# A chunk sum of the attention weights' exps by an accumulating DMA instead of VectorE, with a new order of the work

## The chip, the cores and the metric

One core of one Trainium2 chip. The metric is the device time of the kernel in microseconds (us): 325.75 us, the median of three runs (325.48 to 327.68). A core has five engines that the kernel programs: TensorE (PE in the profile, with its weight loads as PEld), VectorE (DVE), ScalarE (ACT), GpSimd (POOL) and SyncE (SP). Each runs its own instructions in the order in which they were written and waits on semaphores for the others. DMAs are issued by POOL, SP and ACT.

## The reference, cut to what matters

Attention with 16 extra "beacon" keys, then a feed-forward layer with an ELU, over 8 batches, 8 heads, 576 queries, head size 64:

```python
k_all = np.concatenate([beacon_k, k], axis=2)          # 16 + 576 keys
v_all = np.concatenate([beacon_v, v], axis=2)
scores = scale * np.matmul(q, k_all.transpose(0, 1, 3, 2))
scores = np.where(causal, -1000000000.0, scores)       # the beacons are seen by all
scores = scores - scores.max(-1, keepdims=True)
a = np.exp(scores)
a /= a.sum(-1, keepdims=True) + 1e-09
attn = np.matmul(a, v_all)
x = attn.transpose(0, 2, 1, 3).reshape(B * S, H * D)   # 4608 x 512
h = x @ w_in                                           # 512 x 2048
g = np.where(h > 0.0, h, np.exp(np.minimum(h, 0.0)) - 1.0)
return g @ w_out                                       # 2048 x 512
```

What the change touches is `a.sum(-1)`, the denominators of the softmax.

## The kernel before, in words

**The order is a list of words.** The kernel defines steps (`S`, `x`, `m`, `D`, `L` and so on) and then runs a long string of words such as `D.4.0.1` (lines 831 to 958), one step with its arguments each. The order of the words is the order of the instructions on every engine; nothing is reordered afterwards. A word that ends in `.v` runs on VectorE what its plain form runs on ScalarE; one that ends in `.d` gives to a DMA what its plain form gives to VectorE.

**Attention.** For batch b the 592 keys are cut into five chunks of up to 128 (`kc`), and because of the causal mask chunk j is needed only for queries from `ilo[j]` on: 0, 112, 240, 368, 496. So the scores of one head have 576 + 464 + 336 + 208 + 80 = 1664 columns (keys on partitions, queries along the columns). `S` (line 307) multiplies keys with queries into PSUM, `x` (line 328) takes the exp on ScalarE into the tiles `et`, of which there are three in rotation, one per batch and group of four heads. `m` (line 345) zeroes the masked corners on VectorE: part 0 in chunks 0 and 1, part 1 in chunks 2 to 4.

**The denominators.** A sum over keys is a sum over partitions and over chunks. `D.b.d.n` (line 390) adds the chunks of head group d (d = 0 or 1) on VectorE into one tile of fp16, `presum`, which lies in `qkp` and exists once: n = 0 adds chunks 0 and 1 (128 x 1856 elements over four heads), n = 1 adds chunk 2 to that (128 x 1344), n = 2 chunk 3 (128 x 832), n = 3 chunk 4 (80 x 320). `L` (line 408) then multiplies the result with a block of ones on TensorE (line 426); where there is no presum it multiplies each chunk (line 377). `n` (line 436) turns the sums into reciprocals with Ln and Exp on ScalarE, `W` (line 455) multiplies the exps with v, and `M` (line 485) scales the result into `xT` on VectorE. Batches 3 to 7 have `D` for both groups, batch 2 for one, eleven groups in all.

The branch that the change uses is there already, at lines 397 to 400:

```python
if eng == "d":
    nc.gpsimd.dma_start(out=o, in_=t[0:rows, :, col:col + e - a], accum_op=ALU.add)
    return
nc.vector.tensor_tensor(
```

**The feed-forward layer.** Tokens are taken in ten tiles (0 to 9; 256 columns for 0 and 1, then 512). In tiles 0 to 5 `F` (line 509) is four products of 512 columns (L518) that give one bank of h; `e` (L528) takes exp on ScalarE, `u` (L534 on ScalarE, L536 with `.v`) the ReLU, and `k` (L548) joins both on VectorE into `gt`. `r` and `g` (L555, L560) do the same as `u` and `k` by two VectorE instructions. There are two banks for h, so the next `F` but one waits until `e` and `u` have read the bank. Tiles 6 to 9 use a seven-product scheme for the same layer: `P` (L732), `K` (L746, L749), `E` (L760), `U` (L767, L769), `V` (L777), with `X` and `H` making its operands. The second layer uses such a scheme in tiles 1 to 9: `Z` makes combinations of `gt`, `Q.t.a.b` runs products a to b of 112 (L625), `J` copies the results out of PSUM and sends them off. `Z.t.1.B.d` (L571) already is an accumulating DMA in SBUF, of 512 KB; in tiles 3 to 8 some `J` add into the output with an accumulating DMA (L656).

**Queues.** POOL issues the loads of q, k and v (`lq`, `lv`, `lk`), of the weights (`wi`, `wo`) and all accumulating DMAs; `lp` are small copies on POOL. `lk` puts q or k of a later batch into DRAM as bf16, and `lt` (SP, L808) reads it back with a transpose. SP issues most outputs.

Of the kernel before, what the change touches and what calls it, by code (L numbers as in the profile page):

```python
# [17 lines left out]
def kernel(  # L18
# [813 lines left out]
    warm.1 lq.0.0.0.4 warm.1 warm.1 lq.0.1.0.4 warm.4 warm.1 lq.0.0.4.8 warm.1 warm.4 ident  # L832
    warm.1 bt bk T.0.0.0 cb.0.1 warm.1 cb.0.0 cb.0.2 warm.1 ck.0.0.0 lq.0.1.4.8 T.0.1.0 S.0.0.0
    T.0.0.1 cq.0.1.0 S.0.1.0 x.0.0.0 warm.1 cq.0.0.1 T.0.1.1 S.0.0.3 x.0.1.0 T.0.3.0 S.0.0.2
    cq.0.1.1 x.0.0.3 T.0.2.0 cq.0.3.0 lq.1.0.0.4 x.0.0.2 S.0.1.3 x.0.1.3 cb.0.3 warm.1 S.0.1.1
    x.0.1.1 T.0.2.1 S.0.1.2 tri cb.1.1 m.0.0.3 warm.1 x.0.1.2 S.0.3.0 cq.0.2.0 cq.0.2.1 T.0.3.1
    S.0.2.3 lv.0.2 warm.1 lv.0.0.1 x.0.3.0 m.0.3.0 m.0.0.0 x.0.2.3 S.0.2.0 m.0.1.0 x.0.2.0
    m.0.2.0 S.0.0.1 x.0.0.1 wi.2 S.0.2.2 x.0.2.2 L.0.A cb.1.0 T.1.0.0 cq.1.0.0 T.1.1.0 n.0.A
    cq.0.3.1 m.0.2.2 warm.4 S.0.2.1 W.0.A.0 ck.1.1.0 S.0.3.2 lv.0.3.4 x.0.2.1 m.0.1.2 x.0.3.2
    M.0.A.0 W.0.A.1 S.0.3.1 x.0.3.1 wi.1 m.0.2.3 M.0.A.1 S.1.1 cb.1.2 x.1.1 m.0.1.3 m.0.0.2  # L840
    S.0.3.3 F.0.4 x.0.3.3 m.0.3.3 S.1.4 x.1.4 m.0.3.2 e.0.4 L.0.B W.0.B.0 u.0.4.v k.0.4 n.0.B
    S.1.3 F.0.2 M.0.B.0 x.1.3 lq.1.0.4.8 F.0.3 S.1.0 u.0.3.v u.0.2.v W.0.B.1 x.1.0 T.1.2.0
    M.0.B.1 e.0.3 F.0.5 lq.2.0.0.4 m.1.0.0 e.0.2 ck.1.2.0 cb.1.3 T.1.3.0 e.0.5 k.0.2 S.1.6
    cq.1.3.0 wi.0 F.1.5 S.1.2 u.0.5 x.1.6 e.1.5 k.0.3 x.1.2 S.1.5 cb.2.0 k.0.5 F.1.4 S.1.10
    u.1.5.v k.1.5 x.1.5 H.1.0 u.1.4 e.1.4 F.1.2 x.1.10 u.1.2.v k.1.4 e.1.2 T.2.0.0 F.0.1 S.1.7
    e.0.1 wi.3 lv.1.0.1 cq.2.0.0 F.0.0 x.1.7 T.2.1.0 u.0.0 S.1.12 r.0.1 g.0.1 e.0.0 lq.2.0.4.8
    cq.2.1.0 x.1.12 F.1.0 m.1.0.1 cb.2.1 e.1.0 u.1.0.v S.1.11 S.1.9 x.1.11 F.0.6 x.1.9 k.1.2
    u.0.6.v S.1.8 x.1.8 F.1.6 lv.1.2.3.4 e.0.6 k.1.0 u.1.6.v T.2.3.0 T.2.2.0 ck.2.3.0 cb.2.3
    F.0.7 k.0.0 wo.1 S.2.10 e.1.6 F.1.1 cb.2.2 cq.2.2.0 m.1.1.0 m.1.1.1 k.1.6 L.1.0 u.0.7 wo.2
    x.2.10 e.0.7 k.0.7 n.1.0 L.1.1 lp.3.1 M.1.0.0 n.1.1 k.0.6 F.1.3 lp.3.0 M.1.1.0 W.1.1 M.1.1.1  # L850
    e.1.3 u.1.1 W.1.0 u.1.3 M.1.0.1 e.1.1 S.2.4 x.2.4 F.1.7 F.2.8 wo.0 k.1.3 u.1.7 e.1.7 S.2.1
    k.1.1 u.2.8 e.2.8 k.1.7 lp.4.0 S.2.3 x.2.3 wt.1.0 F.2.13 F.2.7 u.2.7 wo.3 S.2.5 k.2.8 lk.3.0
    u.2.13 x.2.1 Z.1.3.B Q.1.0.7 Q.1.7.14 Z.1.1.B lk.3.1 lk.4.0 e.2.7 e.2.13 k.2.7 Q.1.14.21
    Q.1.21.28 x.2.5 Z.1.2.B wt.2.0 J.1.0 F.2.5 e.2.5 S.2.11 wt.3.0 lv.2.0.1 u.2.5 k.2.5
    lv.2.2.3.4 wt.1.1 S.2.6 lk.4.1 wt.2.1 Q.1.28.35 x.2.6 x.2.11 F.2.1 F.2.3 e.2.3 S.2.8 lk.5.0
# [131 lines left out]
```

## Time and profile before

| | |
|---|---|
| median of three runs | 325.75 us |
| the profiled execution's own time | 325.44 us |
| its span in the profile | 323.7 us |
| PE, DVE, ACT, POOL busy | 315.3, 291.9, 291.3, 116.1 us |
| granted TensorE clock | 1.00 of full speed |
| L400, the chunk sums on DVE | 11 each of four shapes: 1118, 849, 585 and 316 ns |

In the views of the profile L400 means line 400 of the kernel. "Busy" counts the time in which an engine executes; DMA issues take time of the engine that issues them. A row of a group gives engine, operation, output and inputs with their shapes, the count, and behind the bar the busy time in us and the mean of one in ns, then the idle time before them and what ended it. A row of the view of DMAs gives the issuing queue, the count, the size of one and the us from its issue to its landing.

### The profile page before, as it was taken

The page shows a single profiled execution, that of the slowest core. Times are in us where ns is not written, and L with a number is a line of the kernel's source. Part 1 is how long each engine was busy: PE and PEld are TensorE (multiplying, and loading weights), DVE is VectorE, ACT ScalarE, POOL GpSimd, SP SyncE. Part 2 cuts the span into 40 slices and gives each one's busy share as a digit, 9 for nine tenths or more (in the row PEclk, how much of TensorE's full clock was granted, in tenths as well). Part 3 has the DMA queues.
Part 4 walks back from the last instruction along what each step waited for, and adds up shares of the span by engine and source line. Part 5 has one row for each costly group of instructions (what it writes and reads, how often), then busy time and mean ns, then how long its engine had stood idle before and what let it go on. Part 6 is the DMA issues. An engine that isn't in the chain of part 4 may idle for free.

```text
span 323.7 us, 9046 instructions
## 1 busy us (share of the span) xinstructions
PE 315.3 (97%) x3705; PEld 224.0 (69%) x3708; DVE 291.9 (90%) x533; ACT 291.3 (90%) x485; POOL 116.1 (36%) x133
## 2 busy tenths in 40 slices
PE   8889999999999999999999999999999999999995
PEld 3557776656556656555655568788888888888884
DVE  2776999999979999989998999999999998989963
ACT  2998999999799999999999998999999999998930
POOL 8984729545247300550155061310401211131110
PEclk9999999999999999999999999999999999999999
DMA  9999999999999999599999992923484292374345
GB/s 113 179 186 204 185 201 165 159 139 172 141 171 174 174 140 177 68 132 148 195 134 136 166 116 62 146 53 93 61 141 99 35 130 59 90 111 73 97 99 130
DMA packets 141657, 42.53 MB, mean 131 GB/s; under 512 B 113200, under 2 KB 141616, under 8 KB 141616
## 3 DMA queue, kind: packets, MB, share of 16 engines
q0 software_dynamic: 106976, 26.35, 90.3%
q1 hardware_dynamic: 33920, 15.34, 24.9%
...
## 4 chain that ended last, share of the span: by engine, by line
PE 83%; ACT 8%; DVE 5%; issue 2%
PE ops L625 29%; PE hps L518 18%; PE hps L732 11%; PE sc L319 6%; PE ut L377 5%; ACT et L334 5%; PE sa L732 4%; PE sx L625 2%; PE w L205 2%; PE lt L377 1%; ACT e L528 1%; DVE gt L573 1%; PE lt L426 1%; DVE qkp L400 1%; PE ub L377 1%
## 5 line engine op out<-in xcount | busy, mean ns | idle before, releaser
L334 ACT ACTIVATE et<-sc 128x1024 f16<-128x1024 f32 (+2 forms) x114 | 104.1, 973 | 3.9 <-PE sc L319 3.5
L625 PEld LDWEIGHTS <-gt 128*128 128x128 f16 x864 | 83.2, 98 | 16.3 <-issue 1.3
L518 PE MATMUL hps<-xT,w_in 128*128 128x512 f16 (+1 forms) x384 | 79.1, 345 | 0.6 <-ACT e L528 0.4
L656 POOL DMA_DIRECT2D out_dram<-osb x18 | 22.0, 1224 | 127.1 <-ACT osb L649 65.8
L518 PEld LDWEIGHTS <-w_in 128*128 128x128 f16 x384 | 34.5, 98 | 28.8 <-issue 5.4
L625 PE MATMUL ops<-w_out,gt 128*128 128x256 f16 x416 | 54.1, 273 | 0.0
L625 PE MATMUL ops<-wt,gt 128*128 128x256 f16 x400 | 52.4, 273 | 0.0
L528 ACT ACTIVATE e<-hps 128x512 f32<-128x512 f32 x80 | 48.6, 625 | 2.1 <-PE hps L518 2.1
L548 DVE SCALAR_TENSOR_TENSOR gt<-e,r 128x512 f16<-128x512 f32 x73 | 48.8, 684 | 1.7 <-ACT e L528 0.8
L777 DVE SCALAR_TENSOR_TENSOR gt<-e,r 128x512 f16<-128x512 f32 x64 | 42.6, 683 | 1.9 <-ACT e L760 1.5
L149 POOL DMA_DIRECT2D v<-in_v_dram x40 | 38.6, 1270 | 7.8 <-issue 4.4
L534 ACT ACTIVATE r<-hps 128x512 f16<-128x512 f32 x55 | 33.1, 627 | 1.4 <-PE hps L518 1.4
L339 DVE TENSOR_TENSOR et<-et,triu 128x1024 f16<-128x1024 f16 (+5 forms) x66 | 26.5, 447 | 2.1 <-ACT et L334 2.1
L760 ACT ACTIVATE e<-qst 128x512 f32<-128x512 f32 x40 | 26.0, 657 | 1.5 <-DVE qst L749 1.5
L732 PEld LDWEIGHTS <-w_in 128*128 128x128 f16 x256 | 24.4, 98 | 4.2 <-issue 0.4
L573 DVE TENSOR_TENSOR gt<-gt 128x2048 f16<-128x2048 f16 (+1 forms) x24 | 25.9, 1084 | 0.2
L377 PEld LDWEIGHTS <-v 128*32 128x32 f16 (+1 forms) x800 | 17.5, 97 | 9.0 <-issue 1.4
L749 DVE TENSOR_TENSOR qst<-hps,kst 128x512 f32<-128x512 f32 x32 | 21.7, 684 | 0.7 <-ACT kst L746 0.6
L377 PE MATMUL ut<-et,v 128*32 128x464 f16 (+3 forms) x560 | 20.9, 296 | 0.1
L571 POOL DMA_DIRECT2D gt<-gt x6 | 9.9, 1658 | 27.2 <-DVE gt L548 20.2
L746 ACT COPY kst<-hps 128x512 f32<-128x512 f32 x32 | 18.7, 603 | 1.1 <-PE hps L732 1.1
L400 DVE TENSOR_TENSOR qkp<-qkp,et 128x1344 f16<-128x1344 f16 (+2 forms) x33 | 19.2, 583 | 0.4
...
## 6 DMA issues: line engine op xcount, KB each, us to landing
out_dram<-sm SPq DMA_DIRECT2D x18, 256.0 KB, 2.7
out_dram<-osb POOLq DMA_DIRECT2D x18, 256.0 KB, 4.3
out_dram<-osb SPq DMA_DIRECT2D x17, 256.0 KB, 5.2
v<-in_v_dram POOLq DMA_DIRECT2D x24, 128.0 KB, 10.5
gt<-gt POOLq DMA_DIRECT2D x6, 512.0 KB, 7.0
scr<-in_q_dram POOLq DMA_DIRECT2D x5, 576.0 KB, 19.8
scr<-in_k_dram POOLq DMA_DIRECT2D x5, 576.0 KB, 21.4
w_in<-in_moe_w_in_dram POOLq DMA_DIRECT2D x8, 256.0 KB, 8.6
```

The lines of the kernel that those rows point to most:

```text
L149: nc.gpsimd.dma_start(out=vt[b][r0:r0 + n, j, :, :], in_=v[b, :, ilo[j]:ilo[j] + n, :].rearrange("h s d -> s h d"),)
L334: nc.scalar.activation(out=ets[b, d][:, :, a - EC2 * d:e - EC2 * d], in_=sc[b, g][:, :, a - c0:e - c0], func=AFT.Exp, bias=0.0, scale=SCALE)
L339: nc.vector.tensor_tensor(out=o, in0=o, in1=i, op=ALU.mult)
L377: nc.tensor.matmul(out=t[32 * i:32 * (i + 1), a - qa:e - qa], lhsT=ones[0:kc[j], :] if half is None else v16[0:kc[j], j, h, half:D:2], rhs ...
L518: nc.tensor.matmul(out=h[:, n_, :], lhsT=w_in16[:, cc, P * fc:P * (fc + 1)], rhs=xt[k][:, cc, a - TT * k:e - TT * k], start=(cc == 0), sto ...
L528: nc.scalar.activation(out=eb[t, i], in_=flat(hp[t, i]), func=AFT.Exp, bias=0.0, scale=1.0)
L534: nc.scalar.activation(out=rb[t, i], in_=flat(hp[t, i]), func=AFT.Relu, bias=0.0, scale=1.0)
L548: nc.vector.scalar_tensor_tensor(out=half(t, i), in0=eb[t, i], scalar=1.0, in1=rb[t, i], op0=ALU.subtract, op1=ALU.min)
L573: (nc.vector if eng == "v" else nc.gpsimd).tensor_tensor(out=o_, in0=a_, in1=b_, op=op_)
L625: nc.tensor.matmul(out=half_of(xy[t, n_], qd), lhsT=lw[:, P * qd:P * (qd + 1)], rhs=wt_[:, c, :], start=(first and c == 0 and (qd == 0 or ...
L732: nc.tensor.matmul(out=hx[t, g, n_][:, c, :], lhsT=lw, rhs=rh, start=(first and c == 0 and k_ == 0), stop=(k_ == 1), skip_group_check=True)
L777: eng.scalar_tensor_tensor(out=o_, in0=v_(eb[t, g, ph]), scalar=1.0, in1=v_(rb[t, g, ph]), op0=ALU.subtract, op1=ALU.min)
```

## The change

Eight words get a `.d`: `D.4.0.1`, `D.4.1.1`, `D.5.0.1`, `D.5.1.1`, `D.6.0.1`, `D.6.1.1`, `D.7.0.1`, `D.7.1.1`. So in batches 4 to 7 chunk 2 of each head group is added by a DMA that POOL issues. The functions are unchanged. The whole list of words is new: the same steps in another order, and some with another engine. Counted over the lists: `u` on ScalarE 55 before and 51 after, `u.v` 18 and 23, `r`/`g` pairs 7 and 6, `k` 73 and 74, `U` 40 and 41, `U.v` 24 and 23, `J` and its `.v` forms with one more on VectorE, and one of the first copies out of PSUM by ScalarE (`ck.0.1.0`) instead of VectorE (`cq.0.1.0`). The lines around batches 4 and 5:

```diff
-    Q.2.91.98 M.3.1.1 u.3.11 e.3.11 M.3.1.0 D.4.0.0 S.5.4 x.5.4 S.4.7 x.4.7 Q.2.98.105 F.4.3
-    S.5.3 S.4.9 k.3.1 J.2.5 e.4.3 u.4.3 D.4.0.1 D.4.0.2 Q.2.105.112 D.4.0.3 F.3.15 k.3.12 k.4.3
...
-    Q.3.35.42 x.5.9 x.5.10 m.4.1.1 m.4.1.0 k.4.14 D.4.1.0 u.4.4 u.4.15 e.4.15 Q.3.42.49 S.5.0
-    S.5.5 F.4.0 k.4.4 F.4.6 lt.6.1 x.5.5 x.5.0 e.4.6 W.4.1 u.4.0 H.4.2 e.4.0 D.4.1.1 D.4.1.2
-    D.4.1.3 H.4.0 k.4.15 J.3.2 L.4.1 m.5.0.1 Q.3.56.63 m.5.0.0 Q.3.63.70 u.4.6 k.4.6 n.4.1
...
+    Q.2.77.84 J.2.4 u.3.0 F.3.4 k.3.13 u.3.4 D.4.0.1.d lp.6.0 Q.2.84.91 F.3.15 e.3.4 M.3.1.0
+    M.3.1.1 k.3.0 F.3.11 e.3.15 u.3.15 S.4.9 S.4.11 F.3.12 lk.6.0 lt.5.1 lp.5.1 x.4.9 Q.2.91.98
+    u.3.11.v k.3.15 S.4.12 u.3.12.v x.4.11 e.3.11 H.4.0 k.3.11 S.5.3 Q.2.98.105 F.4.2 x.4.12
+    e.3.12 k.3.4 D.4.0.2 F.3.1 x.5.3 e.4.2 S.4.8 S.4.7 u.3.1 Q.2.105.112 e.3.1 u.4.2.v F.4.11
...
+    F.4.12 F.4.9 k.4.7 lk.7.0 u.4.9.v D.4.1.0 u.4.12 Q.3.14.21 e.4.12 S.5.11 S.5.7 e.4.9 k.4.12
+    F.4.4 F.4.10 D.4.1.1.d x.5.11 S.5.2 x.5.7 k.4.9 u.4.4.v e.4.10 lv.5 lt.6.0 S.5.0 e.4.4
+    u.4.10.v J.3.0 Q.3.21.28 Z.3.2.B F.4.14 k.4.8 Q.3.28.35 x.5.0 F.4.0 x.5.2 J.3.1 S.5.8 k.4.4
+    S.5.6 k.4.10 D.4.1.2 D.4.1.3 Q.3.35.42 e.4.0 x.5.8 x.5.6 Q.3.42.49 Q.3.49.56 S.5.1 u.4.14
...
+    x.5.1 S.5.10 x.5.10 r.4.0 g.4.0 m.5.0.1 m.5.0.0 Q.3.56.63 F.4.15 L.4.1 e.4.15 D.5.0.0
+    D.5.0.1.d lt.6.1 e.4.14 k.4.14 u.4.15.v W.4.1 J.3.2 F.4.13 n.4.1 M.4.1.0 Q.3.63.70 F.4.6
+    M.4.1.1 J.3.3 lk.7.1 e.4.13 S.6.2 S.5.12 u.4.13 e.4.6 F.4.5 k.4.15 u.4.6 Q.3.70.77 F.4.1
...
+    Q.3.84.91 F.5.13 x.5.9 S.6.3 J.3.4.v x.6.4 x.6.3 S.6.1 k.4.1 F.5.14 Q.3.91.98 D.5.0.2
+    D.5.0.3 m.5.1.0 L.5.0 x.6.1 D.5.1.0 u.5.13 e.5.13 H.4.2 W.5.0 n.5.0 m.5.1.1 F.5.12
+    Q.3.98.105 u.5.14 M.5.0.1 M.5.0.0 e.5.12 e.5.14 Q.3.105.112 u.5.12 X.6.1 F.5.15 k.5.14
+    F.5.10 D.5.1.1.d k.5.12 S.6.9 J.3.5 u.5.15 S.6.6 Z.4.3.B Z.4.1.B.d J.3.6.v e.5.15 F.5.7
...
```

The order of POOL's words in the stretch that has them, before:

```
lk.5.0 lv.3.2.3.4 lv.3.0.1 lp.4.1 lk.5.1 lk.7.0 lp.5.0 lk.6.1 lv.4 lk.6.0 lp.5.1
Z.3.1.B.d lv.5 lk.7.1 lp.6.0 J.3.1 lp.7.0 lp.6.1 J.3.4.v J.3.5 Z.4.1.B.d lv.6
lp.7.1 J.4.1.v lv.7 J.4.4 Z.5.1.B.d
```

and after:

```
lp.3.1 lv.3.2.3.4 lk.5.0 lv.3.0.1 lk.5.1 lk.6.1 lv.4 lp.5.0 lp.4.1 D.4.0.1.d lp.6.0
lk.6.0 lp.5.1 Z.3.1.B.d lp.6.1 lk.7.0 D.4.1.1.d lv.5 J.3.1 D.5.0.1.d lk.7.1 J.3.4.v
D.5.1.1.d J.3.5 Z.4.1.B.d lp.7.0 lv.6 D.6.0.1.d J.4.1.v lp.7.1 lv.7 D.6.1.1.d J.4.4
Z.5.1.B.d
```

At the start, `ident` comes after the first four loads instead of the first six, and 13 of the `warm` products (matmuls of zeros) stand ahead of `bt` instead of 14.

More of the change, by code (lines that the diff above doesn't have):

```diff
@@ L831 @@
     run("""
[L832 to L855, printed above, removed]
@@ L952 @@
-    V.9.2.4 U.9.3.5 K.9.3.4 E.9.3.1 E.9.3.5 P.9.3.6 V.9.3.1 V.9.3.5 U.9.2.6 Q.8.84.91 U.9.3.4.v
-    J.8.4 Z.9.3.0 Q.8.91.98 Q.8.98.105 Q.8.105.112 E.9.3.6 Z.9.1.0 E.9.3.4 V.9.3.4 U.9.3.6
-    E.9.2.6 V.9.3.6 J.8.6 Z.9.3.1 Q.9.0.7 V.9.2.6 Z.9.1.1 Q.9.7.14 Q.9.14.21 Z.9.2.1 Z.9.2.0
-    Q.9.21.28 J.9.0 Q.9.28.35 J.9.1 Q.9.35.42 Q.9.42.49 Q.9.56.63 Z.9.4.0 J.9.2 Q.9.49.56
-    Q.9.63.70 Q.9.70.77 J.9.3.v Q.9.77.84 Z.9.4.1 J.8.5 Q.9.84.91 J.9.4 Q.9.91.98 J.9.5
+    warm.4 warm.1 lq.0.0.0.4 lq.0.1.0.4 warm.4 ident warm.4 bt bk lq.0.0.4.8 warm.1 warm.1
@@ new lines @@
+    T.0.0.0 ck.0.0.0 warm.1 cb.0.3 cb.0.0 T.0.1.0 ck.0.1.0 S.0.0.0 T.0.0.1 cb.0.1 cq.0.0.1
+    x.0.0.0 S.0.1.0 T.0.1.1 S.0.0.2 cq.0.1.1 T.0.3.0 x.0.1.0 S.0.1.3 T.0.2.0 x.0.0.2 lq.0.1.4.8
+    S.0.1.1 cb.0.2 cq.0.2.0 warm.1 warm.1 lq.1.0.0.4 cq.0.3.0 x.0.1.3 S.0.1.2 T.0.2.1 cq.0.2.1
+    x.0.1.1 lv.0.2 x.0.1.2 S.0.0.3 x.0.0.3 warm.1 warm.1 S.0.3.0 T.0.3.1 x.0.3.0 cq.0.3.1
+    S.0.2.2 lv.0.0.1 x.0.2.2 warm.1 cb.1.1 S.0.2.3 warm.1 x.0.2.3 tri m.0.1.0 S.0.2.0 x.0.2.0
+    m.0.0.3 S.0.3.2 warm.1 S.0.3.1 warm.1 x.0.3.2 x.0.3.1 S.0.0.1 x.0.0.1 S.0.3.3 x.0.3.3
@@ new lines @@
+    K.6.0.5 M.6.0.0 V.6.0.6 J.4.6 P.6.1.1 H.4.3 S.7.3 K.6.1.0 E.6.0.5 S.7.12 x.7.3 P.6.1.2
+    Q.5.0.7 K.6.1.1 V.6.0.1 P.6.1.3 U.6.1.1.v K.6.1.2 S.7.2 P.6.1.4 Q.5.7.14 E.6.1.1 D.6.1.2
+    K.6.1.3 x.7.2 U.6.0.5.v P.6.1.5 D.6.1.3 K.6.1.4 V.6.0.4 V.6.0.5 P.6.1.6 L.6.1 K.6.1.5 x.7.12
+    W.6.1 E.6.1.6 n.6.1 U.6.1.4.v P.6.2.0 U.6.1.6 K.6.2.0 V.6.1.1 Q.5.14.21 E.6.1.4 P.6.2.1
+    E.6.1.5 P.6.2.2 U.6.1.5.v M.6.1.1 M.6.1.0 V.6.1.4 K.6.2.1 J.5.0 S.7.4 K.6.2.2 S.7.5
+    Q.5.21.28 E.6.2.1 x.7.4 P.6.2.4 Z.5.2.B V.6.1.6 P.6.2.3 K.6.2.3 Q.5.28.35 Q.5.35.42 P.6.2.5
@@ new lines @@
+    K.8.2.0 K.8.1.5 P.8.2.1 V.8.0.4 V.8.1.1 J.7.0 P.8.2.2 P.8.2.3 E.8.1.6 E.8.2.1 Q.7.21.28
+    U.8.2.1.v U.8.1.6 U.8.1.5.v K.8.2.2 V.8.1.6 P.8.3.3 P.8.3.0 E.8.1.4 K.8.2.3 Z.7.2.B V.8.2.1
+    U.8.1.4 P.8.2.4 P.8.2.5 K.8.2.5 E.8.1.5 Q.7.28.35 J.7.1 K.8.2.4 E.8.2.5 X.9.1 K.8.3.3
+    K.8.3.0 Q.7.35.42 V.8.1.5 Q.7.42.49 P.8.2.6 E.8.2.6 Q.7.56.63 P.8.3.1 P.8.3.2 U.8.2.4
+    V.8.1.4 Z.7.4.B P.8.3.5 U.8.2.5 K.8.3.2 E.8.2.4 U.8.2.6 Q.7.49.56 J.7.2.v V.8.2.5 Q.7.63.70
+    P.9.0.0 K.8.3.5 V.8.2.4 P.8.3.4 J.7.3.v Q.7.70.77 Q.7.77.84 E.8.3.1 U.8.3.5 K.8.3.4 X.9.2
@@ L957 @@
+    E.9.3.5 V.9.3.5 E.9.3.4 V.9.2.6 Q.8.84.91 Q.8.91.98 P.9.3.6 U.9.3.6 E.9.3.6 Z.9.3.1 J.8.5
+    Q.9.0.7 V.9.3.4 V.9.3.6 Q.8.98.105 Q.8.105.112 J.8.6 Z.9.1.1 Q.9.7.14 Z.9.2.0 Q.9.14.21
+    Z.9.2.1 Q.9.21.28 J.9.0 Q.9.28.35 J.9.1 Z.9.4.0 Z.9.4.1 Q.9.35.42 Q.9.42.49 Q.9.49.56
+    J.9.2.v Q.9.56.63 Q.9.63.70 J.9.3.v Q.9.70.77 Q.9.77.84 Q.9.84.91 J.9.4 Q.9.91.98 J.9.5
     Q.9.98.104 Jh.9.0 Q.9.104.112 Jh.9.1
```

178 lines of the change are left out of this document (87 added, 91 removed).

## The prediction

> **What bounds the kernel now.** I read the page first: engine shares, slices, the chain that ended last.
>
> ```profile
> span 323.7 us, 9046 instructions
> PE 315.3 (97%) x3705; PEld 224.0 (69%) x3708; DVE 291.9 (90%) x533; ACT 291.3 (90%) x485; POOL 116.1 (36%) x133
> ...
> DMA  9999999999999999599999992923484292374345
> ...
> PE 83%; ACT 8%; DVE 5%; issue 2%
> ```
>
> Three engines are near full, TensorE most, and the DMA engines are full up to slice 24 (some 194 us) except for one slice. An average doesn't say where TensorE waits, so the busy time by stretch comes next: start, length, busy us of PE, PEld, DVE, ACT, POOL, then clock, DMA share, GB/s.
>
> ```profile
> 0.00:20.00 20.00, 16.83 (x255) 9.52 (x258) 11.08 (x36) 12.84 (x17) 17.69 (x31) 1.00 1.34 152
> 20.00:40.00 20.00, 19.28 (x371) 13.78 (x371) 16.30 (x37) 18.76 (x28) 13.02 (x21) 1.00 1.46 195
> 40.00:60.00 20.00, 19.43 (x337) 12.87 (x336) 18.72 (x34) 18.79 (x29) 11.22 (x12) 1.00 1.74 178
> ```
>
> ```profile
> 60.00:280.00 220.00, 219.83 (x2388) 152.71 (x2386) 212.11 (x374) 213.13 (x360) 66.73 (x65) 1.00 1.19 126
> ```
>
> ```profile
> 150.00:250.00 100.00, 100.00 (x1124) 73.05 (x1123) 98.44 (x183) 98.33 (x170) 26.86 (x28) 1.00 0.91 117
> ```
>
> ```profile
> 300.00:323.70 23.70, 20.16 (x184) 17.64 (x182) 15.09 (x26) 10.01 (x21) 2.35 (x2) 1.00 0.45 108
> ```
>
> TensorE is idle for 3.2 + 0.7 + 0.6 us in the first 60, for 0.17 us in the next 220, and for 3.5 us in the tail. Busy could hide stalls, so I look at the chain of work around the first affected batches (start, length, what).
>
> ```profile
> 142.93 1.83 PE hps L518 x8
> 144.76 0.76 PE ops L625 x7
> 145.53 0.55 PE sc L319 x12
> ```
>
> Seven L625 products in 0.76 us are 109 ns each; 256 columns at that pace are 2.35 per ns, and the granted clock is 1.00 in every row above. Eight L518 products of 512 columns in 1.83 us are 229 ns each, the same pace with one transition. So from 60 us on TensorE streams at its rate: this kernel is **bound by TensorE**, with VectorE and ScalarE, 98% busy at 150 to 250 us, just able to feed it.
>
> **The change, part by part.** The prices of what leaves and joins VectorE, by group and shape:
>
> ```profile
> L400 DVE TENSOR_TENSOR qkp<-qkp,et 128x1344 f16<-128x1344 f16 x11 | 9.3, 849 | 0.0
> L548 DVE SCALAR_TENSOR_TENSOR gt<-e,r 128x512 f16<-128x512 f32 x73 | 48.8, 684 | 1.7 <-ACT e L528 0.8 <-ACT r L534 0.7
> L536 DVE TENSOR_SCALAR r<-hps 128x512 f16<-128x512 f32 x18 | 12.3, 689 | 4.9 <-ACT e L528 3.2 <-PE hps L518 1.2
> L560 DVE TENSOR_TENSOR gt<-hps,r 128x512 f16<-128x512 f32 x7 | 4.8, 688 | 0.2
> L555 DVE TENSOR_SCALAR r<-e 128x512 f16<-128x512 f32 x7 | 3.6, 521 | 0.1
> L534 ACT ACTIVATE r<-hps 128x512 f16<-128x512 f32 x55 | 33.1, 627 | 1.4 <-PE hps L518 1.4
> ```
>
> *Removed:* eight sums of 128x1344 at 849 ns, 6.8 us of VectorE. *Given back by the new order:* counting words of both lists, five more `u` with `.v` (18 to 23) at 689 ns, +3.4; one `r`/`g` pair fewer, -1.2, and its `k`, +0.7; the other swaps (two `U.v` fewer, one `U.6.v` and one `J.v` more, one `cq` fewer) nearly cancel. VectorE nets some -3.9 us; ScalarE, with four `u` fewer at 627 ns, about -2. TensorE's matmuls are the same in number and shape. Since TensorE lacks only 0.17 us between 60 and 280 us, the relief has almost nothing to buy there: I take **0** of it, bounds 0 and the 0.6 + 0.17 us idle between 40 and 280. What covers the eight sums today is TensorE's stream.
>
> *Added:* eight DMAs of 128 x 1344 x 2 bytes, 336 KB, from SBUF into SBUF with an add, issued by POOL, on the queue that also carries the loads of v, q and k. The trace has no such transfer of this size; the nearest rows (size, median us to landing; then the six 512 KB ones: ns of the issue, and landing min/median/max):
>
> ```profile
> out_dram<-osb POOLq DMA_DIRECT2D x18, 256.0 KB, 4.3
> v<-in_v_dram POOLq DMA_DIRECT2D x24, 128.0 KB, 10.5
> gt<-gt POOLq DMA_DIRECT2D x6, 512.0 KB, 7.0
> scr<-in_q_dram POOLq DMA_DIRECT2D x5, 576.0 KB, 19.8
> scr<-in_k_dram POOLq DMA_DIRECT2D x5, 576.0 KB, 21.4
> ```
>
> ```profile
> L571 POOL DMA_DIRECT2D gt<-gt x6: 1532/1562/2164, 133.4 to 285.6; - x6
> ...
> DMA to landing us min/median/max: 6.4/7.0/10.0
> ```
>
> Between 4.3 us at 256 KB and 7.0 at 512 lies 4.3 + 80/256 x 2.7 = **5.1 us** for 336 KB, an estimate; with the worst `gt` instead, 8.1. POOL's own cost is 8 x 1.6 = 12.5 us of an engine that is 36% busy; it delays nothing but what stands behind it in POOL's order.
>
> The Trainium skill's page "DMA: Bandwidth & Descriptors" (section "Anatomy of one DMA") gives 2.0 us plus bytes over 436 GB/s. By that rule ours would land in 2.8 us, and the 512 KB ones in 3.2; the trace shows 6.4 to 10.0 for these, so the rows decide. By the page no wait would ever appear, and the sum would be the second case below.
>
> *The new wait.* `D.b.d.2` adds into the tile that the DMA writes, so VectorE stops at it until the DMA has landed, and queued behind it are `k`, `u.v` and copies that free TensorE's banks. Prices of TensorE's words, from the chain of work:
>
> ```profile
> 158.44 0.86 PE hps L518 x4
> 191.86 1.32 PE ut L377 x40
> 194.50 0.87 PE hps L732 x8
> ```
>
> An `F` is four L518, 0.86 us; a `P` four L732, 0.44; a `Q` product 0.109; an `S` about 0.45 and a `W` about 1, estimated from the L319 row above and the L377 row, which hold more than one word. Between `D.b.d.0`, after which the DMA can go, and `D.b.d.2` the new list has this much TensorE work: 10.8, 8.5, 12.7, 9.0, 16.0, 10.6, 13.5 and 8.3 us for 4.0, 4.1, 5.0, 5.1, 6.0, 6.1, 7.0, 7.1. By VectorE's words alone it is 7.4, 5.4, 8.0, 7.7, 13.8, 7.4, 11.7 and 7.7. All exceed 5.1, nearly all 8.1. On a free queue this change **waits nowhere**.
>
> The queue isn't free. A tiny transfer behind a large one shows it (issues at 96 to 99 us, and one scr load on a nearly empty queue at 47.4 us):
>
> ```profile
> scr<-in_k_dram POOLq DMA_DIRECT2D x1, 576.0 KB, 23.0
> v<-in_beacon_v_dram POOLq DMA_DIRECT2D x1, 16.0 KB, 21.5
> ```
>
> ```profile
> scr<-in_q_dram POOLq DMA_DIRECT2D x1, 576.0 KB, 11.0
> ```
>
> 16 KB took 21.5 us, because what POOL issued before had to go first. So each new DMA is read with its predecessors in POOL's order: 4.0 follows `lk.5.1 lk.6.1 lv.4`, long issued; 4.1 stands **right behind `lk.7.0`**; 5.0 behind the six pieces of `lv.5`; 5.1 behind `lk.7.1`; 6.0 and 6.1 behind `lv.6` and `lv.7`, but with 16.0 and 10.6 us; 7.0 and 7.1 behind nothing. The critical one is 4.1. Its time in the present run:
>
> ```profile
> 133.38 1.58 POOL L571 DMA_DIRECT2D gt<-gt  x1 [20.23 <-DVE gt L548]
> ```
>
> ```profile
> 148.29 1.11 DVE L400 TENSOR_TENSOR qkp<-et 128x1856 f16<-128x1856 f16 x1
> ```
>
> The new list has four `F`, 28 `Q` products and six `S` less ahead of `D.4.1.0`: 3.5 + 3.1 + 2.7 = 9.3 us, so it starts near 139.0 and ends at 140.1; `D.4.1.2` is then due at 148.6. `lk.7.0` waits behind `Z.3.1.B.d` (133.4 now) and goes at about 135. It lands after 11.0 us (146) to 23.0 (158); our 336 KB behind it add 336/256 x 2.7 = 3.5: 149.5 to 161.5. VectorE is late by 0.9 to 12.9 us; I take 2.5, near the low end, because in the new list the transposing reads and `lv.5`, which run beside the k load at 139 us now, come after `lk.7.0`. TensorE has 21 `Q` products (2.3 us) and two `S` there that ask nothing of VectorE, so about 0.7 us of it passes through. For 5.0 and 5.1, whose margins over 8.1 are 4.6 and 0.9, I add 0.5 together (0 to 3).
>
> *Moved:* everything else. The start is limited by loads and ScalarE:
>
> ```profile
> 10.72 7.67 ACT et L334 x10
> ```
>
> Ten exps in a row there; the new list puts `ident` two DMAs earlier on POOL (earlier first transposes, later second half of the q and k loads), gives ScalarE one more copy (`ck.0.1.0`) ahead of the first exp and has 13 `warm` ahead of `bt` instead of 14. I take 0, bounds -1.5 and +2: the idle 3.2 us of the first row can't all go.
>
> *Sum.* The profiled execution took 325.44 us (span 323.7 and 1.7 around it), 0.3 below the median of 325.75: 325.4 + 0 + 0.7 + 0.5 = **326.6 us**. A change of under 1% (3.3 us) is about what can't be told from none here.
>
> **The rivals.**
>
> *No wait at all (325.3).* All eight DMAs land in time; TensorE's stream sets the end. For it: the margins above; the six `gt` transfers, for which VectorE waits nowhere: the only DMA among what it waited for is the first load.
>
> ```profile
> DVE hi L219 <- DMA lo<-in_beacon_k_dram: 3.7, 1, 3.7
> ```
>
> Against: the scr load just ahead of 4.1. With part of the idle 0.8 us: 324.6 to 325.4. The skill's DMA page, by its 2.8 us, gives this case.
>
> *The queue ahead of 4.1 (331.5, slower).* `lk.7.0` lands as the scr loads mostly do, in 20 to 23 us: 4.1 lands at 158.5 to 161.5, VectorE is 10 to 13 us late. The cover of 2.3 us and 3.9 us of relieved VectorE come off, which leaves 4 to 7, say 5, and 5.0 and 5.1, behind `lv.5` and `lk.7.1` in the same backlog, add about 1: 325.4 + 6 = 331.5, up to 333. It decides from the point where VectorE's wait at `D.4.1.2` exceeds about 6 us, that is, a landing after 154.6.
>
> *The start gains (322.4, faster).* 1.5 us from the start, 0.8 from the idle rest, 0.7 off the tail's 3.5: 325.4 - 3.0. Against: three engines have to be early at once.
>
> *The sums leave VectorE in name only.* VectorE stands at `D.b.d.2` for as long as the sum took (0.85 us each): 6.8 us of waits replace 6.8 of work, and the five added `u.v` make it 3.4 longer than now; TensorE covers most: +1, inside the forecast's range.
>
> **How the numbers follow.** Forecast, with the last rival in it: 0.50, own range 325.0 to 328.9. No wait: 0.15. Queue: 0.27. Start: 0.08. Faster by over 1%: 0.08; within: 0.65; slower: 0.27. The range leaves out the start's gain and the worst of the queue: 323.6 to 332.0.
>
> **What would show it.** Right: L400 of 128x1344 at three instead of eleven; eight new POOL issues into qkp, landing in 5 to 8 us from batch 6 on and later in 4.1; idle time of VectorE before L400 put down to that DMA, under 3 us each; TensorE's 60 to 280 us at 218 or more of 220. Wrong: VectorE waits of 6 us and more, with L518 behind them waiting for e or r; or a first L518 shifted by over 2 us.

## The result and the profile after

The changed kernel takes **331.32 us** (median of 17 runs, 327.01 to 337.80) against 325.75 (17 runs, 325.41 to 327.68). The ratio, with the five longest, disturbed runs of the changed kernel left out, is **1.0105 (95% interval 1.0082 to 1.0129)**: slower by about 1%, just at the bound named in the prediction. The medians over all 17 lie further apart, 1.7%. The profiled execution is the longest of the 17 (337.8 us), so its rows show the loss at its largest; there is no profile of an execution near the median. Run 7 below, whose list behind the start is the same, gives a second look at the same places.

From the page of the changed kernel, the rows that answer to the first ones of before:

```profile
span 336.1 us, 9064 instructions
...
PE 318.5 (95%) x3708; PEld 224.3 (67%) x3708; DVE 289.0 (86%) x531; ACT 289.4 (86%) x479; POOL 127.5 (38%) x141
...
PEclk9999999999999999999999995999999999999999
DMA  9999999999999929999979999963592666466362
...
PE 75%; ACT 9%; DMA 8%; DVE 3%; issue 2%; POOL 2%; ACTq 0%; DVEq 0%; POOLq 0%
```

VectorE lost 2.9 us of work and ScalarE 1.9, POOL gained 11.4. New is the share of DMA in the chain that ended last, 8%, and the one slice (202 to 210 us) with half the TensorE clock. The stretches (start, length, busy us of PE, PEld, DVE, ACT, POOL, clock, DMA share, GB/s):

```profile
20.00:40.00 20.00, 17.66 (x411) 12.99 (x401) 13.31 (x24) 17.72 (x27) 13.29 (x21) 1.00 1.48 194
60.00:150.00 90.00, 90.00 (x946) 53.27 (x945) 83.63 (x141) 86.44 (x136) 34.87 (x36) 1.00 1.64 153
150.00:180.00 30.00, 30.00 (x356) 17.96 (x357) 26.60 (x47) 28.82 (x49) 14.67 (x14) 1.00 1.44 149
180.00:210.00 30.00, 22.39 (x214) 13.55 (x203) 20.21 (x42) 18.90 (x31) 8.12 (x10) 0.89 1.79 134
210.00:280.00 70.00, 69.95 (x780) 58.43 (x778) 68.81 (x126) 67.34 (x124) 18.18 (x14) 1.00 0.66 101
```

So in this execution the loss has two main places. From 20 to 40 us TensorE is busy 17.66 us where it was 19.28: 1.6 us. From 180 to 210 us it is idle for 7.6 us, at a mean clock of 0.89. Between 60 and 180 us, where the DMAs of 4.0, 4.1, 5.0 and 5.1 are, and after 210 us, TensorE is as full as before.

The sums and their DMAs, by group and by line:

```profile
L400 DVE TENSOR_TENSOR qkp<-qkp,et 128x1344 f16<-128x1344 f16 x3 | 2.6, 851 | 0.0
L400 DVE TENSOR_TENSOR qkp<-qkp,et 128x832 f16<-128x832 f16 x11 | 6.5, 587 | 8.5 <-DMA qkp<-et 8.4
...
L536 DVE TENSOR_SCALAR r<-hps 128x512 f16<-128x512 f32 x23 | 15.6, 684 | 1.9 <-ACT e L528 0.9 <-PE hps L518 0.6
```

```profile
L398 POOL DMA_DIRECT2D qkp<-et x8: 1287/1304/1326, 122.5 to 257.8; - x8
...
  DVE qkp L400: 8.4, 4
...
DMA to landing us min/median/max: 4.9/6.7/21.6
```

Eight sums are gone from VectorE, and eight DMAs are there. They land in 4.9 to 8.9 us, all but one: the DMA of 6.0 takes **21.6 us**. Of the 8.4 us that VectorE waits for them, 5.9 are at that one. The waits from 170 to 212 us (in total, times, longest):

```profile
DVE qkp L400 <- DMA qkp<-et: 5.9, 1, 5.9
...
PE lt L426 <- DVE qkp L400: 4.2, 1, 4.2
...
DVE gt L573 <- DMA gt<-gt: 2.0, 1, 2.0
PE ops L625 <- DVE gt L573: 2.0, 1, 2.0
...
PE ut L377 <- DMA v<-in_v_dram: 1.4, 1, 1.4
```

TensorE's three waits add up to the 7.6 us: 4.2 behind the DMA of 6.0, 2.0 behind `gt` and 1.4 for v, and all three transfers are among those of the stretch from 173 to 182 us. What TensorE does around it, in stretches of 5 us (the sixth of the figures after the length is the granted clock):

```profile
195.00:200.00 5.00, 3.57 (x56) 1.84 (x54) 2.42 (x8) 4.46 (x7) 4.78 (x7) 1.00 1.43 131
200.00:205.00 5.00, 0.78 (x24) 0.40 (x16) 1.64 (x6) 0.00 (x0) 0.20 (x1) 0.77 2.23 112
205.00:210.00 5.00, 5.00 (x33) 3.54 (x26) 3.34 (x7) 2.41 (x4) 0.00 (x0) 0.54 1.51 175
210.00:215.00 5.00, 5.00 (x48) 4.47 (x46) 4.41 (x10) 3.64 (x8) 3.86 (x3) 1.00 0.71 73
```

It stands for 4.2 us, and then runs at 0.54 of its clock for 5 us: it looks full there, and does 33 matmuls where the next stretch has 48. At 0.54 those 5 us are worth 2.7, so the slow clock adds 2.3 us to the wait. By the sum 1.6 + 7.6 + 2.3 = 11.5 of the 12.4 us between the two spans are placed.

The 9.9 us at 180 to 210 are those of the longest execution, not the price of this place in the ratio. In the profile of run 7 (328.87 us), with the same order there, the DMA of 6.0 takes 15.1 us, and the stretch costs TensorE 1.5 us at full clock:

```profile
180.00:210.00 30.00, 28.52 (x294) 20.05 (x287) 28.09 (x62) 26.32 (x45) 13.06 (x13) 1.00 1.54 161
```

Why 6.0? The DMAs in flight from 173 to 181 us, changed kernel (size, median us to landing):

```profile
gt<-gt POOLq DMA_DIRECT2D x1, 512.0 KB, 11.9
v<-in_v_dram POOLq DMA_DIRECT2D x3, 128.0 KB, 14.3
...
qst<-scr SPq DMA_TRANSPOSE x2, 13.0
```

and the same transfers from 160 to 175 us in the kernel before:

```profile
gt<-gt POOLq DMA_DIRECT2D x1, 512.0 KB, 10.0
v<-in_v_dram POOLq DMA_DIRECT2D x3, 128.0 KB, 9.4
...
qst<-scr SPq DMA_TRANSPOSE x2, 5.8
```

The difference is on SP's queue. SP from 155 us on, changed kernel, then the kernel before (start, us, what):

```profile
174.14 0.37 SPq L654 DMA_DIRECT2D out_dram<-osb  x1
174.62 6.05 SPq L808 DMA_TRANSPOSE qst<-scr  x2
```

```profile
160.30 4.57 SPq L808 DMA_TRANSPOSE qst<-scr  x2
176.99 0.37 SPq L654 DMA_DIRECT2D out_dram<-osb  x1
```

In the old list `lt.7.0`, the transposing read of batch 7, stands ahead of `J.3.6.v`, whose output SP writes, and runs at 160 us. In the new list it stands behind it, and SP gets to it at 174.6 us: just when POOL issues `gt`, the six pieces of `lv.6` and, at 181.7 us, the DMA of 6.0. That this bunching makes the landing late was a reading so far; the runs test it.

### The profile page after: what moved, and what is told of

The parts are those of the page before. It is cut to its first block, busy times and chain, and to the rows that moved or that the text cites. A ratio compares the mean times of both kernels' runs of the same rounds, so it can differ in the third digit from the quotient of the medians.

```text
span 336.1 us, 9064 instructions
## 1 busy us (share of the span) xinstructions
PE 318.5 (95%) x3708; PEld 224.3 (67%) x3708; DVE 289.0 (86%) x531; ACT 289.4 (86%) x479; POOL 127.5 (38%) x141
## 4 chain that ended last, share of the span: by engine, by line
PE 75%; ACT 9%; DMA 8%; DVE 3%; issue 2%; POOL 2%; ACTq 0%; DVEq 0%; POOLq 0%
PE ops L625 29%; PE hps L518 16%; PE hps L732 11%; DMA qkp<-et 6%; PE sc L319 6%; PE ut L377 5%; ACT et L334 4%; PE sa L732 4%; PE sx L625 2%; DMA kst<-in_k_dram 2%; ACT e L528 2%; PE lt L377 1%; ACT r L534 1%; PE lt L426 1%; POOL qst L136 1%
## 5 line engine op out<-in xcount | busy, mean ns | idle before, releaser
L518 PE MATMUL hps<-xT,w_in 128*128 128x512 f16 (+1 forms) x384 | 80.3, 344 | 0.0
L625 PE MATMUL ops<-wt,gt 128*128 128x256 f16 x400 | 53.4, 273 | 2.0 <-DVE gt L573 2.0
L149 POOL DMA_DIRECT2D v<-in_v_dram x40 | 37.2, 1113 | 10.4 <-issue 5.2
L534 ACT ACTIVATE r<-hps 128x512 f16<-128x512 f32 x51 | 31.0, 623 | 2.7 <-PE hps L518 2.3
L398 POOL DMA_DIRECT2D qkp<-et x8 | 10.4, 1305 | 55.5 <-PE hps L518 24.5
L760 ACT ACTIVATE e<-qst 128x512 f32<-128x512 f32 x40 | 25.2, 646 | 1.7 <-DVE gt L777 0.8
L377 PEld LDWEIGHTS <-v 128*32 128x32 f16 (+1 forms) x800 | 17.1, 97 | 10.6 <-DMA v<-in_v_dram 1.7
L400 DVE TENSOR_TENSOR qkp<-qkp,et 128x832 f16<-128x832 f16 (+2 forms) x25 | 12.5, 500 | 8.7 <-DMA qkp<-et 8.4
```

What stands on the lines that cost most here:

```text
L149: nc.gpsimd.dma_start(out=vt[b][r0:r0 + n, j, :, :], in_=v[b, :, ilo[j]:ilo[j] + n, :].rearrange("h s d -> s h d"),)
L377: nc.tensor.matmul(out=t[32 * i:32 * (i + 1), a - qa:e - qa], lhsT=ones[0:kc[j], :] if half is None else v16[0:kc[j], j, h, half:D:2], rhs ...
L518: nc.tensor.matmul(out=h[:, n_, :], lhsT=w_in16[:, cc, P * fc:P * (fc + 1)], rhs=xt[k][:, cc, a - TT * k:e - TT * k], start=(cc == 0), sto ...
L534: nc.scalar.activation(out=rb[t, i], in_=flat(hp[t, i]), func=AFT.Relu, bias=0.0, scale=1.0)
L625: nc.tensor.matmul(out=half_of(xy[t, n_], qd), lhsT=lw[:, P * qd:P * (qd + 1)], rhs=wt_[:, c, :], start=(first and c == 0 and (qd == 0 or ...
```

## The experiments

Theory A: the loss is the bunching in batch 6 and the new start. Rivals: the order of POOL's queue alone; a loss of the order everywhere. Each run gives the median and the ratio to the kernel before in the same group of runs; where two runs come from different groups, their ratios are compared and not their times.

**1. The order without the DMAs.**

```diff
- D.4.0.1.d ... D.7.1.1.d     (eight words)
+ D.4.0.1   ... D.7.1.1
```

> The new order with all eight sums back on VectorE, no new DMA. Theory A (about 1.7 us are lost at 20 to 40 us by the new order itself, the rest, which differs from run to run, by the new DMA of 6.0 behind v of batch 6): 327.2 to 328.0 us, with a small spread, and TensorE 19.9 of 20 busy from 180 to 220 us. Rival B (the new order costs everything, its transposing reads of batch 7 beside v of batch 6 included): 329 to 333 us with the spread of the changed kernel, and TensorE idle again between 185 and 205 us.

332.75 us (331.92 to 333.89), ratio 1.0216 (1.0169 to 1.0262). So the order by itself is **slower** than the kernel before, and slower than with its DMAs (1.0082 to 1.0129). A's range was missed; the time is that of the rival, a loss of the order. No single place carries it. Its page, and its stretch from 60 to 280 us:

```profile
PE 317.7 (96%) x3706; PEld 223.6 (68%) x3708; DVE 294.1 (89%) x539; ACT 290.1 (88%) x479; POOL 115.5 (35%) x133
```

```profile
60.00:280.00 220.00, 217.54 (x2336) 147.62 (x2335) 210.34 (x372) 207.65 (x346) 64.75 (x66) 1.00 1.16 123
```

TensorE is idle for 2.5 us of 220, in waits of at most 0.5 us. That is 2.3 us more than before, of 6.5 between the spans (330.2 and 323.7); 1.1 more lie from 20 to 40 us, and the rest is not placed. VectorE has 294.1 us of work, 2.2 more than before. The likely reading, which no run isolates, is that the new order gives VectorE more to do and counts on the DMAs to take it back.

**2. 6.0 alone back on VectorE.**

```diff
- D.6.0.1.d
+ D.6.0.1
```

> The changed kernel with the one sum D.6.0.1 back on VectorE, seven DMAs left. Theory A: 327.2 to 328.5 us, VectorE's longest wait for a chunk sum under 2 us. Rival C (every one of the eight waits costs its part): seven eighths of the loss beyond the start stay, 329 to 331 us. Rival B: as the changed kernel, 329 to 333.

328.46 us (328.28 to 332.80), ratio 1.0105 (1.0036 to 1.0173). In its profile seven DMAs cost VectorE 1.4 us of waits in all, the longest 0.7, and TensorE is busy 28.97 us of the 30 from 180 to 210 where the changed kernel has 22.39. Without the DMA of 6.0 the long stall is gone. Its price in the median does not follow: the ratio equals the changed kernel's, with a wide interval.

**3. `lv.6` behind the DMA of 6.0.**

```diff
- lv.6 ... D.6.0.1.d
+ D.6.0.1.d lv.6
```

> The changed kernel with one word moved: the loads of v for batch 6 are issued behind the DMA of D.6.0.1 instead of ahead of it. Theory A: this DMA lands in under 12 us instead of 21.6 and VectorE no longer waits for it; 327.2 to 329 us, unless W of batch 6 then waits for v, which would show as TensorE waiting for v by 1 to 3 us. Rival D (the transposing reads beside it, not its place in POOL's queue, make it late): it still lands after 18 us or more, 329 to 333.

330.40 us (330.01 to 330.80), ratio 1.0132 (1.0101 to 1.0164). The DMA of 6.0 now lands in 5.4 us, and the wait moves to what was put behind it. TensorE's waits from 180 to 212 us, and one stretch:

```profile
PE ut L377 <- DMA v<-in_v_dram: 2.1, 2, 1.2
```

```profile
195.00:200.00 5.00, 2.87 (x53) 1.38 (x46) 2.58 (x9) 2.18 (x4) 1.96 (x3) 0.73 1.87 163
```

The place on POOL's queue decides who is late, not that someone is late. The transposing reads still run from 174.3 us in this profile, and `gt` still goes ahead, so these without `lv.6` do not make the DMA late. The clock of 0.73 is worth a look: it fell to 0.50 in the second of two waits, of 0.9 and 1.2 us with four short products between them, and stayed there for 3.4 us.

**4. The DMAs in the old order.**

```diff
- D.4.0.1   ... D.7.1.1     (old list)
+ D.4.0.1.d ... D.7.1.1.d
```

> The old order with the same eight sums given to the DMA, nothing else moved. There D.b.d.2 follows within 0 to 5 us of VectorE's work. With a landing after 5 to 9 us VectorE waits some 3 to 6 us at each of the eight, 30 us in all, of which TensorE covers about 2 each: theory A 335 to 345 us. Rival E (TensorE's stream hides the landing wherever the word stands): 325 to 328 us.

381.45 us (379.00 to 382.54), ratio 1.1687 (1.1632 to 1.1743), far above what either theory gave. In the old list `D.4.0.2` stands right behind `D.4.0.1`:

```profile
L400 DVE TENSOR_TENSOR qkp<-qkp,et 128x832 f16<-128x832 f16 x11 | 6.5, 589 | 55.6 <-DMA qkp<-et 55.5
```

```profile
160.00:170.00 10.00, 0.00 (x0) 0.00 (x0) 0.00 (x0) 0.97 (x2) 2.94 (x4) 0.64 1.65 177
170.00:180.00 10.00, 7.21 (x56) 4.46 (x57) 6.78 (x14) 3.72 (x7) 0.00 (x0) 0.67 0.14 20
```

VectorE waits 55.5 us over seven DMAs, up to 14.6 at one. Of the 57.1 us between the spans (380.8 and 323.7), 43.7 are more idle time of TensorE and 13.4 more busy time, at a mean clock of 0.94. So the old list has no slack into which these landings fit, and a list that takes the DMAs needs another order.

**5. `lt.7.0` early, with `lk.7.1` ahead of the DMA of 5.0.**

```diff
- D.4.1.2 ... D.5.0.1.d ... lk.7.1 ... D.5.1.0 ... J.3.6.v ... lp.7.0 ... lv.6 lt.7.0
+ D.4.1.2 lk.7.1 ... D.5.0.1.d ... D.5.1.0 lp.7.0 lt.7.0 ... J.3.6.v ... lv.6
```

> The changed kernel, but the second k load of batch 7 (lk.7.1) is issued behind D.4.1.2 instead of behind D.5.0.1.d, and the transposing reads of q of batch 7 (lp.7.0, lt.7.0) stand behind D.5.1.0, ahead of the write of J.3.6 on SP's queue, so that they run near 160 us as in the kernel before and not at 174 to 191 beside lv.6 and D.6.0.1.d. Theory A (bunching: the DMA of 6.0 lands late because gt, six v pieces and four transposing reads are in flight with it): D.6.0.1.d lands in under 10 us, lv.6 in under 12, VectorE waits under 1.5 us for it, 327.5 to 328.8 us. Theory B (the queue alone: gt and lv.6 ahead of it on POOL's queue are enough): it still takes 15 us or more, VectorE waits 4 us or more, 330.5 to 331.5.

334.61 us (333.44 to 337.09), ratio 1.0256 (1.0209 to 1.0304). Both theories missed the time, because the edit made a new stall. The landing went as A said: 6.0 in 7.4 us instead of 21.6. But the 576 KB of `lk.7.1` now go just ahead of the DMA of 5.0. The two at 155 us, and the waits from 150 to 185:

```profile
scr<-in_k_dram POOLq DMA_DIRECT2D x1, 576.0 KB, 14.3
qkp<-et POOLq DMA_DIRECT2D x1, 336.0 KB, 14.5
```

```profile
DVE qkp L400 <- DMA qkp<-et: 7.0, 1, 7.0
...
PE lt L426 <- DVE qkp L400: 5.7, 1, 5.7
```

That is the rival "the queue ahead" of the prediction, at another sum.

**6. The new start alone**, the first 210 words of the new list before the rest of the old, no DMA of a sum:

```diff
- (words 1 to 210 of the old list)
+ (words 1 to 210 of the new list)
```

> The kernel before, with the first 210 words (some 45 us) in the new order and all that follows in the old one; no sum is made by DMA. Theory A (the start of the new order costs 0.5 to 1.8 us by itself, TensorE waiting for S.1.3 near 32 us): 326.9 to 327.9 us. Theory B (the start's loss is noise between executions): 325.5 to 326.4, TensorE's work done by 40 us within 0.5 us of the kernel before.

Words that the old start has and the new one has not yet, such as `H.1.0`, follow at the join; run 7 does the like.

329.71 us (328.63 to 332.36), ratio 1.0103 (1.0066 to 1.0141): more than A said. TensorE's waits from 20 to 60 us:

```profile
PE hps L518 <- ACT e L528: 1.5, 1, 1.5
PE sc L319 <- DVE r L555: 1.4, 1, 1.4
```

The second is in the changed kernel too (1.7 us), and not in the one before. The first, at 51.6 us, is not in the changed kernel and comes behind the join of the two lists, so this run overstates the start.

**7. The old start with the rest of the new list.**

```diff
- (words 1 to 210 of the new list)
+ (words 1 to 210 of the old list)
```

> The changed kernel with the first 210 words in the old order; the eight DMAs and the rest of the new order stay. Theory A: the start's 1.5 us come back and the late landing of 6.0 stays: 328.8 to 330.2 us, a VectorE wait of 3 us or more at D.6.0.2. Theory B (start is noise): 331 to 331.8.

331.31 us (328.87 to 333.32), ratio 1.0136 (1.0086 to 1.0185). The wait of 1.7 us is gone (TensorE busy 19.28 us from 20 to 40, as before), and the median does not move. What the start is worth in the median isn't settled by this, since the join of the two lists brings a wait of its own at 49 us, which is 0.2 us in the changed kernel:

```profile
PE lt L377 <- DVE hi L278: 0.7, 1, 0.7
```

TensorE is busy 18.82 us from 40 to 60, where the changed kernel has 19.55.

**8. Old start, with the edit of run 5.**

```diff
- (words 1 to 210 of the new list); lk.7.1, lp.7.0, lt.7.0 late
+ (words 1 to 210 of the old list); lk.7.1, lp.7.0, lt.7.0 as in run 5
```

> Both edits together: first 210 words in the old order, and lk.7.1, lp.7.0 and lt.7.0 earlier; all eight sums still by DMA. Theory A (start and bunching are the whole loss): 325.7 to 327.0 us, within 1% of the kernel before, no VectorE wait over 1.5 us for a DMA of a sum. Theory C (the new order loses spread out through batches 2 to 7, whatever the start and the landings): 328 to 329.5.

335.01 us (333.68 to 336.45), ratio 1.0252 (1.0213 to 1.0291): run 5 again, with 5.0 landing in 14.4 us and 6.0 in 7.3. Both of its expectations were missed, by the stall at 5.0.

**9. `lt.7.0` early, with the small copy `lp.7.0` beside it, and nothing else.** The separation that run 5 missed:

```diff
- J.3.4.v ... J.3.6.v ... lp.7.0 ... lv.6 lt.7.0
+ lp.7.0 lt.7.0 J.3.4.v ... J.3.6.v ... lv.6
```

> The changed kernel, with lp.7.0 and lt.7.0 alone moved up, ahead of J.3.4.v; lk.7.1 stays behind D.5.0.1.d, so no load is put ahead of the DMA of 5.0. The transposing reads then run at 158 to 173 us, not beside lv.6 and the DMA of 6.0. Theory A (bunching): D.6.0.1.d lands in under 10 us, 5.0 in 9 as now, VectorE waits under 1.5 us for any DMA of a sum, 327.5 to 329 us. Theory B (gt and lv.6 ahead on the queue are enough): D.6.0.1.d takes 15 us or more, 330.5 to 331.5.

**328.01 us** (327.07 to 329.50), ratio 1.0074 (1.0048 to 1.0100), as A said. SP, then the DMA of 6.0, issued at 181.5 us with the same `gt` and `lv.6` ahead of it on POOL's queue:

```profile
157.55 14.56 SPq L808 DMA_TRANSPOSE qst<-scr  x2
```

```profile
qkp<-et POOLq DMA_DIRECT2D x1, 336.0 KB, 6.9
```

From 21.6 to 6.9 us by moving one pair of transposing reads on another queue; the pieces of v fall from 14.3 to 8.3 us, `gt` from 11.9 to 8.7. That **bunching makes the landing late is shown**, and the queue alone is refuted: run 10 against run 7, both with the old start, repeats it (7.1 against 15.1 us). By run 3 the reads are not enough without the loads of `lv.6` ahead; it takes both. What it is worth in time is not shown: the interval of this run overlaps with the changed kernel's. The rest of this profile:

```profile
20.00:40.00 20.00, 17.77 (x412) 13.06 (x396) 13.47 (x25) 17.83 (x27) 13.57 (x21) 1.00 1.50 194
...
60.00:280.00 220.00, 219.96 (x2379) 151.54 (x2378) 209.38 (x371) 211.24 (x355) 76.72 (x74) 1.00 1.26 137
```

With all eight sums on DMAs TensorE is idle for 0.04 us of 220. What is left of the loss in this execution, the fastest of the six, is the start: 19.28 - 17.77 = 1.5 us, of the 1.7 between the spans (325.4 and 323.7).

**10. The same with the old start.**

> The same, and the first 210 words in the old order. If the start and the landing of 6.0 are the whole loss: 325.8 to 327.2 us. If the rest of the new order loses by itself: 328 to 329.5, with TensorE's work falling behind that of the kernel before outside of 20 to 40 and 180 to 210 us.

```diff
- (words 1 to 210 of the new list)
+ (words 1 to 210 of the old list, with the edit of run 9)
```

328.91 us (327.63 to 329.34), ratio 1.0092 (1.0068 to 1.0115): not better than run 9, and in the range of the expectation that the rest of the new order loses by itself. The wait of the start is gone, but in the profiled execution the clock is lower there, which no edit explains (it fell to 0.50 at 17.5 us, with waits of at most 0.4 us in the 3 us before, and stayed there for 3.4 us):

```profile
0.00:20.00 20.00, 17.56 (x246) 9.88 (x248) 9.89 (x35) 12.38 (x16) 17.83 (x31) 0.94 1.35 152
```

Two more places lose: the join, as in run 7 (18.82 us busy from 40 to 60), and 150 to 180 us, where the DMA of 5.0 takes 10.7 us, VectorE waits 2.0 for it and TensorE is busy 29.31 of 30.

So all seven profiles with the new start show a wait at `S.1.3` of 0.8 to 1.7 us, none with the old start does, and yet the old start did not win it back in the median. The join takes back a part; how much of the rest is the new order itself stays open.

**11. One sum by DMA in the old order**, its followers moved away from it:

```diff
- D.7.0.1 ... D.7.0.2 ... D.7.0.3 ... J.6.0 L.7.0
+ D.7.0.1.d ... J.6.0 D.7.0.2 D.7.0.3 L.7.0
```

> The kernel before in its own order, with one sum, D.7.0.1, by DMA and its followers D.7.0.2 and D.7.0.3 moved behind J.6.0, so that some 7 us of TensorE's work stand between. If a sum by DMA is free where it lands in time, and VectorE's 0.85 us buy nothing since TensorE sets the end: 325.5 to 326.4 us (the kernel before within its own spread), landing near 5 us, VectorE waits under 0.5 us. If the DMA costs by itself (POOL's issue, traffic): 327 us or more.

331.85 us (331.19 to 333.58), ratio 1.0194 (1.0168 to 1.0220). Not free: 512 KB of `gt` go 1.8 us ahead of it on POOL's queue, and it lands in 9.5 us. VectorE waits 3.5 us, TensorE 4.5, and then its clock halves:

```profile
240.00:245.00 5.00, 0.78 (x20) 0.55 (x24) 1.75 (x4) 2.30 (x5) 0.00 (x0) 0.83 0.73 148
245.00:250.00 5.00, 5.00 (x56) 2.91 (x49) 2.94 (x5) 1.07 (x2) 0.00 (x0) 0.50 0.02 3
```

A wait of 3.5 us of VectorE costs some 6 us of time.

**12. The same, with `gt` behind the sum's DMA** and the followers two `P` earlier:

```diff
- Z.6.1.B.d ... D.7.0.1.d ... P.7.1.5 P.7.1.6 J.6.0 D.7.0.2 D.7.0.3 L.7.0 ... Z.6.2.B ... m.7.1.1 V.7.1.6
+ D.7.0.1.d Z.6.1.B.d ... D.7.0.2 D.7.0.3 P.7.1.5 P.7.1.6 J.6.0 L.7.0 ... m.7.1.1 V.7.1.6 Z.6.2.B
```

> The old order with the one sum D.7.0.1 by DMA, as in the run before it, but with the DMA of gt (Z.6.1.B.d, 512 KB) issued behind the DMA of the sum and not ahead of it (its follower Z.6.2.B one place later), and D.7.0.2 and D.7.0.3 ahead of P.7.1.5. If what stands ahead on POOL's queue decides the landing, and a sum by DMA on a free queue is free and buys nothing: it lands in 4.8 to 6 us, VectorE and TensorE wait under 0.7 us, no stretch of lower clock, 325.4 to 326.8 us. If the old order itself leaves no room for it: a wait of 2 us or more again, with a lower clock behind it, 329 us or more.

328.98 us (median of 12; 327.65 to 333.96 without one of 527.03), ratio 1.0083 (1.0058 to 1.0108), between the two expectations. The DMA lands in 6.3 us and VectorE waits 0.3, but TensorE still waits 1.2 us at `L.7.0`, and 1.3 at the products behind `Z.6.2.B`, whose `gt` is now the late one: it lands after 9.3 us, at 243.9, and VectorE starts on it at once. The same stretch as above:

```profile
240.00:245.00 5.00, 2.83 (x64) 1.85 (x64) 4.62 (x8) 3.85 (x8) 0.00 (x0) 1.00 0.97 144
```

TensorE is idle for 2.2 us of these five, in parts of two waits, and keeps its clock: 1.00 here and in the next stretch. VectorE's 0.85 us bought nothing.

No version beats the kernel before.

## Why the prediction was right, and where it wasn't

It forecast 326.6 us with a range of 323.6 to 332.0, and no change beyond 1% as the likeliest; 331.32 lies in the range, near its upper end, and the ratio of 1.0105 at the bound. It lies outside the forecast's own 325.0 to 328.9: what held it is the part of the range that was there for the rival of the queue, whose cause did not come. That is luck. The mechanism was right in kind: the sums' price on VectorE buys nothing, and what counts is when a DMA lands. Two of its steps failed, and a third was missing. Of its own signs, three sums instead of eleven and eight new issues came; but VectorE's longest wait was 5.9 us and not under 3, and in the profiled execution TensorE was busy 212.3 us of the 220 from 60 to 280, not 218 (run 7: 218.18).

*TensorE is the bound, the relief is worth 0:* held. VectorE lost 2.9 us (forecast 3.9), ScalarE 1.9 (forecast 2). In run 9, where nothing stalls, TensorE's 219.96 us of 220 are as full as before and the kernel is no faster. What the step left out is that the order needs the relief: without it the same order has a ratio of 1.0216 (run 1), with it 1.0105. The 1.1% between are not a gain on the kernel before; they repay what the order cost.

*5.1 us to land, 8.1 at worst:* five of the eight land in 4.9 to 6.9 us in the changed kernel, two in 7.2 and 8.9. The worst case failed: 21.6. (The 8.1 adds to 5.1 the whole 3.0 us by which the worst `gt` is later than the median one; read between 4.3 and 10.0 us as the 5.1 was, it would be 6.1.)

*"6.0 and 6.1 behind lv.6 and lv.7, but with 16.0 and 10.6 us":* **this step failed**. The margin was right (VectorE came to the sum 15.7 us after the issue), the landing was not. For 4.1 I reckoned with transposing reads beside a load; for 6.0 I read POOL's order alone. The 21.6 us come from its predecessors together with what ran beside it on SP's queue, a pair of transposing reads from 174.6 us, which the new order had moved behind a write that waits for a result of TensorE, and a second pair from 184.8. Run 9 moved the first pair back and the landing fell to 6.9 us behind the same predecessors; run 3 took `lv.6` from ahead of it, left `gt` and the reads, and it fell to 5.4.

*The critical one is 4.1, behind `lk.7.0`:* this failed too, harmlessly. `lk.7.0` landed in 10.0 us (11.0 to 23.0 forecast), 4.1 in 6.5, VectorE waited 1.5 us instead of 2.5, and TensorE, 90.00 us of 90 from 60 to 150, lost none of the 0.7. 5.0 and 5.1 cost 0 where 0.5 was added.

*The start at 0, between -1.5 and +2:* in the profile it cost 1.6 us, a wait at `S.1.3`. The row names VectorE's `r`, but `S.1.3` stands ahead of that `r` in the list, and in runs 2 and 5 it starts before the `r` has ended; what it waits for is not shown. The cost is inside the bounds. The sum with it would have been 328.2, and that run 9 has 328.01 is chance, since the 0.7 and 0.5 in this sum cost nothing there; without them it is 327.0, and the profiled execution of run 9 took 327.07.

*Missing: the clock.* I priced a wait as its length. A stall of 4.2 us cost TensorE 2.3 us more in lower clock. The Trainium skill's page "TensorE: Matmul & The Clock Gate" (section "Part 1: The HAM clock gate") states that an idle window of about 3.4 us drops the clock to half. The traces agree for long waits: those of 4.2 us in the changed kernel, 4.5 in run 11 and 5.7 in run 5 were followed by 0.50, while one of 2.0 us in the changed kernel (at 187 us) and two of 1.2 in run 12 left 1.00. They differ in runs 3 and 10, where the clock fell to 0.50 without a wait of more than 1.2 and 0.4 us.

*The rivals:* "The queue ahead of 4.1" gave 331.5 (its terms, 325.4 + 6, give 331.4), the measured time, with another sum and another cause. Its mechanism exists: run 5 put a k load ahead of 5.0, and the DMA took 14.5 us. "No wait at all", 325.3, is how TensorE stands in run 9 from 60 us on; its median is 2.7 us higher, of which its profile places 1.5 in the start. "The start gains" had the wrong sign. "In name only" did not come as a rule: where nothing was late, in run 9, VectorE waited 1.3 us for DMAs of sums, not the 6.8 of the work.
